# Attention then a cosine-gated MLP on one core: three score tiles to a visit in three rotating PSUM slots, each quad's AV product in one burst, and the last MLP pair of a stage in halves

## The chip, the cores and the metric

The kernel runs on one core of one Trainium2 chip. The metric is the device time of one execution in microseconds; lower is better. A core has five engines that run their own instruction streams and wait for each other through semaphores: TensorE (PE: matrix products, with PEld for its weight loads), ScalarE (ACT), VectorE (DVE), GpSimd (POOL) and SyncE (SP, here only a queue that issues DMAs).

## The reference

```
q, k, v: (8, 12, 448, 64) float32;  tau = 0.1
q_n = q / (norm(q) + 1e-6);  k_n = k / (norm(k) + 1e-6)
attn = softmax(q_n @ k_n.T / tau)             per batch and head, 448 x 448
x = (attn @ v), heads joined                  (3584, 768)
h = x @ w_in                                  (768, 2048)
out = (h * cos(h)) @ w_out                    (2048, 768), float32
```

## The kernel before

**Units.** A *quad* is four heads of one batch element; there are 24 quads (NQ), three per batch element (QB). Its keys are cut into 7 blocks of 64 (NJ). One *score event* `scores(g)` (L551) is four 64x64 matmuls (L560) that fill two neighbouring PSUM banks, and one ScalarE exponential over 128x896 (L567) that writes the tile E[g % NE]. One *AV step* `attend(g)` (L570) is four 64x64 matmuls (L577) that multiply such a tile with V and accumulate over the 7 blocks in banks X and Y (4 and 5); after the seventh, VectorE copies them to AVs (L586). `sums` (L630) gets the softmax denominators of two quads with 128x32 matmuls (L642) into one bank; ScalarE inverts them with a logarithm and an exponential into Zs (L649, L651), sends them to a scratch tensor in DRAM (rscr, L652), SP's queue reads them back spread over partitions (R, L658), and GpSimd multiplies AVs by R into xT (L662; for quad 5 VectorE does).

**Getting q and k ready.** `norm_a` squares q and k on GpSimd (L450) and sums them on VectorE (L454); `norm_b` takes the inverse norm on ScalarE (L480 to L493) and scales q and k on GpSimd (L501); `turn` transposes both with DMAs on SP's queue (L544), from quad 4 on. Loads of q and k are also on SP's queue, those of v and the weights on GpSimd's, the output's stores on SP's.

**The MLP.** A batch element is a *stage* c, 0 to 7. MLP-in: eight pairs of 128 hidden units, twelve matmuls each (`m1_part`, L676, 128x448) into a pair of banks; `m1` (L683) makes h*cos(h) of both at once with two ScalarE and two VectorE operations (L689, L691, L693, L695) into gT. MLP-out (`m2`, L698): for every tile of 128 tokens and half of the columns, 16 matmuls (L704, 128x384) into bank 6 or 7, copied out by VectorE (L722) and stored. A stage has 6 or 8 such half tiles, so 96 or 128 of these matmuls. cos runs on another ScalarE table than the exponential; `table` (L371) loads the one that is needed.

**Order.** TensorE runs in the program's order. The first three quads run ahead of the MLP; the others are spread over the MLP-out phases of stages 0 to 5 (`QUADS`, L731: 5, 4, 3, 3, 3, 3 quads). There the main loop (L916 to L989) lays out the half tiles' matmuls in `items`; `fill(n)` emits n of them, and between the fills `group` (L754) emits a *visit*: one score event, then `flush_av` (L739), which does the AV steps of the visit before, then the second score event. Seven events make four visits per quad. Score events alternate between two slots, bank pairs 0 and 2. For two output tiles at once (three in the last two stages) the first 16 matmuls are cut at 0, 10, 12, 14 and interleaved (`cuts`, L945). The order on the other four engines is not written out: `Planner` (L22) lays all operations out in time with the estimated durations that each `op` call gives, and takes from it each engine's order and the semaphore waits. `lead` makes an operation more urgent, `keep` holds a queue to the program's order.

The AV step of a stage's last visit is flushed in the next stage's MLP-in phase (L934).

Of the kernel before, what the change touches and what calls it, by code (L numbers as in the profile page):

```python
# [271 lines left out]
def bass_cosine_attention__then__act_gcu_kernel(  # L272
# [19 lines left out]
    FIRST = 3  # L292
# [11 lines left out]
    NE, NV, NA = 17, 4, 4  # L304
# [17 lines left out]
    Zs = ring("Zs", 2, [128, S], F32)  # L322
# [228 lines left out]
    def scores(g):  # L551
# [3 lines left out]
        u, bs, es = qd % 2, 2 * (g % 2), g % NE  # L555
# [14 lines left out]
    def attend(g):  # L570
# [17 lines left out]
    Z, LEAD = 6, 15.0  # L588

    def spread(qd, j0, j1):  # L590
# [14 lines left out]
        if j1 < NJ:  # L605
            return
        summed.add(qd)
        act("exp", 0.815, lambda e: e.activation(ar[s].ap(), two(Z), ACT.Ln, bias=0.0, scale=1.0), r=pair(Z), w=[("ar", s)])
        act("exp", 0.83, lambda e: e.activation(ar[s].ap(), ar[s].ap(), ACT.Exp, bias=0.0, scale=-1.0),  # L609
            r=[("ar", s)], w=[("ar", s)])  # L610

    def scale_x(qd):
        b, c0, s = qd // QB, 2 * (qd % QB), qd % 3
        op("dve", 1.01, lambda e: e.tensor_tensor(xT[b % 2].ap()[:, c0:c0 + 2, :], two(X), ar[s].ap(), ALU.mult),
           r=pair(X) + [("ar", s)], w=[("x", b % 2, qd % QB)])
# [12 lines left out]
    rounds, spared = [0], []  # L628

    def sums(quads, bk):  # L630
# [3 lines left out]
        z = n % 2  # L634
# [3 lines left out]
        def mm(e):  # L638
# [9 lines left out]
        zz = Zs[z].ap()[0:32 * np_, :]  # L648
        act("exp", 0.44, lambda e: e.activation(zz, bank(bk, S, 0, 32 * np_), ACT.Ln, bias=0.0, scale=1.0),  # L649
            r=whole(bk), w=[("Zs", z)], lead=LEAD)  # L650
        act("exp", 0.47, lambda e: e.activation(zz, zz, ACT.Exp, bias=0.0, scale=-1.0), r=[("Zs", z)], w=[("Zs", z)], lead=LEAD)  # L651
        op("act", 0.6, lambda e: e.dma_start(rscr.ap()[8 * n:8 * n + rows, :], Zs[z].ap()[0:32 * np_:16, :]),  # L652
           r=[("Zs", z)], w=[("rs", n)], dma=("rs", z), moves=0.05, lead=LEAD)
        for i, qd in enumerate(quads):
            u, sl, b = qd % 2, qd % NA, qd // QB
            for r in range(2):
# [5 lines left out]
            op("dve" if late else "pool", 1.02 if late else 2.04, lambda e, u=u, sl=sl, b=b, c0=c0: e.tensor_tensor(  # L662
                xT[b % 2].ap()[:, c0:c0 + 2, :], AVs[sl].ap(), R[u].ap(), ALU.mult),
                r=[("AV", sl), ("R", u, 0), ("R", u, 1)], w=[("x", b % 2, qd % QB)], lead=LEAD)
# [18 lines left out]
    def m1(c, pr, bk):  # L683
# [3 lines left out]
        bs = pair(bk)  # L687
# [3 lines left out]
        op("dve", 1.005, lambda e: e.scalar_tensor_tensor(ar[s].ap(), ar[s].ap().bitcast(I32), -2.0 * math.pi, two(bk),  # L691
# [334 lines left out]
```

## Time and profile before

| what | value |
|---|---|
| time, median of 3 runs | 441.71 us (440.83 to 442.9) |
| the profiled execution | 441.8 us, of which its span is 439.6 us |
| granted TensorE clock over the span | 0.992 |
| score matmuls L560 | x672, 62.1 us busy |
| AV matmuls L577 | x672, 50.4 us busy |
| MLP-in matmuls L676 | x768, 147.7 us busy |
| MLP-out matmuls L704 | x896, 163.4 us busy |
| exponentials L567 | x168, 916 ns each |
| copies of AV sums L586 | x21, 1087 ns each |

Busy times of TensorE overlap each other, since matmuls are pipelined; the distance between the starts of neighbouring ones is what each takes of the queue. The span falls into a start (to 38.6 us, the first three quads) and eight stages, each an MLP-in phase of about 18.5 us and an MLP-out phase of 17 to 43 us, the first six of which contain the attention of later quads.

### The profile page before, as it was taken

To read this page: it belongs to the slowest core of one execution; us is meant where nothing else is said; L and a number is where in the kernel's file an instruction comes from. 1 tells how busy PE (TensorE), PEld (TensorE's weight loads), DVE (VectorE), ACT (ScalarE), POOL (GpSimd) and SP (SyncE) were. 2 spreads that over 40 slices of the span, in tenths; PEclk is the share of its full clock that TensorE was granted. 3 is DMA by queue.
4 is the path that set the end of the run, shared out by engine and by line. 5 is a ranking of instruction groups with operands and counts; after the bars stand their busy time and mean duration, and the time that the engine had idled before them with its cause. 6 is when DMAs were issued, how large, how long until landed. Compare 5 with 4: busy or idle time off the path is not lost.

```text
span 439.6 us, 8369 instructions
## 1 busy us (share of the span) xinstructions
PE 420.1 (96%) x3544; PEld 204.6 (47%) x3544; DVE 254.7 (58%) x300; ACT 315.3 (72%) x434; POOL 211.2 (48%) x145
## 2 busy tenths in 40 slices
PE   5989999988999999999999999999999999999996
PEld 5444543324544345434554444434454445555553
DVE  4674995347863449823696419923585237825931
ACT  4798789896788877788688667888678666815700
POOL 3878727869167694376637682148633120030000
PEclk9699999999999999999999999999999999999999
DMA  7999996999919969188933994075912611051022
GB/s 253 233 251 227 261 196 92 233 223 208 146 41 240 240 172 213 37 206 123 265 89 80 241 210 141 1 171 150 259 35 48 154 43 30 0 159 36 1 71 73
DMA packets 70941, 64.34 MB, mean 146 GB/s; under 512 B 40100, under 2 KB 63224, under 8 KB 70904
## 3 DMA queue, kind: packets, MB, share of 16 engines
q1 hardware_dynamic: 57824, 51.30, 46.6%
q0 software_dynamic: 12288, 11.80, 18.2%
q10 hardware_dynamic: 792, 0.71, 0.5%
q8 instruction: 28, 0.46, 0.4%
q14 instruction: 9, 0.07, 0.1%
HBM read 55.25 MB, written 11.16 MB: 151 GB/s over the span
## 4 chain that ended last, share of the span: by engine, by line
PE 83%; ACT 9%; DVE 3%; issue 2%; POOL 2%; ACTq 1%; POOLq 0%
PE PS L676 33%; PE PS L704 31%; PE PS L560 7%; PE PS L577 6%; ACT E L567 6%; PE PS L642 4%; DVE n L454 1%; ACT Zs L651 1%; ACT Zs L649 1%; ACTq L652 1%; PE PS L599 1%; PE PS L623 1%; POOL xT L662 0%; DVE gT L695 0%; ACT ar L609 0%
## 5 line engine op out<-in xcount | busy, mean ns | idle before, releaser
L704 PE MATMUL PS<-W,gT 128*128 128x384 bf16 x896 | 163.4, 327 | 1.1 <-DVE osb L722 1.0
L567 ACT ACTIVATE E<-PS 128x896 bf16<-128x896 f32 x168 | 144.8, 916 | 27.0 <-PE PS L560 23.8
L676 PE MATMUL PS<-xT,W 128*128 128x448 bf16 x768 | 147.7, 353 | 1.2 <-POOL xT L662 1.2
L704 PEld LDWEIGHTS PS<-W,gT 128*128 128x128 bf16 x896 | 80.1, 98 | 80.7 <-issue 29.0
L676 PEld LDWEIGHTS PS<-xT,W 128*128 128x128 bf16 x768 | 74.3, 98 | 72.0 <-POOL xT L662 1.6
L689 ACT ACTIVATE ar<-PS 128x896 int32<-128x896 f32 x64 | 58.2, 910 | 45.1 <-PE PS L676 45.1
L691 DVE SCALAR_TENSOR_TENSOR ar<-ar,PS 128x896 f32<-128x896 int32 x64 | 69.2, 1083 | 29.0 <-ACT ar L689 29.0
L722 DVE COPY osb<-PS 128x384 f32<-128x384 f32 x54 | 29.2, 554 | 86.6 <-PE PS L704 86.5
L662 POOL TENSOR_TENSOR xT<-AVs,R 128x896 bf16<-128x896 f32 x20 | 41.4, 2088 | 67.5 <-DMA R<-rscr 67.4
L695 DVE TENSOR_TENSOR gT<-PS,ar 128x896 bf16<-128x896 f32 x64 | 69.6, 1088 | 1.5 <-ACT ar L693 1.0
L693 ACT ACTIVATE ar<-ar 128x896 f32<-128x896 f32 x64 | 60.6, 946 | 13.1 <-DVE ar L691 13.1
L560 PE MATMUL PS<-qT,kT 64*64 64x448 bf16 x672 | 62.1, 368 | 4.9 <-ACT E L567 4.0
L450 POOL TENSOR_TENSOR sqq<-Qf 128x896 bf16<-128x896 f32 x21 | 35.3, 1679 | 49.3 <-DVE n L454 40.9
L577 PE MATMUL PS<-E,Vb 64*64 64x448 bf16 x672 | 50.4, 353 | 2.1 <-ACT E L567 1.8
L501 POOL TENSOR_TENSOR Qn<-Qf,rr 128x896 bf16<-128x896 f32 x21 | 35.4, 1687 | 29.6 <-ACT rr L493 25.1
L450 POOL TENSOR_TENSOR sqk<-Kf 128x896 bf16<-128x896 f32 (+1 forms) x22 | 36.5, 1659 | 25.9 <-DVE n L454 17.9
L586 DVE COPY AVs<-PS 128x896 f32<-128x896 f32 x21 | 22.8, 1087 | 29.6 <-PE PS L577 29.6
L501 POOL TENSOR_TENSOR Kn<-Kf,rr 128x896 bf16<-128x896 f32 (+1 forms) x22 | 37.5, 1705 | 0.5 <-DVE Qn L501 0.5
L560 PEld LDWEIGHTS PS<-qT,kT 64*64 64x64 bf16 x672 | 18.6, 105 | 38.4 <-issue 15.6
L454 DVE TENSOR_REDUCE n<-sqq 128x14 f32<-128x896 bf16 (+2 forms) x24 | 24.9, 1037 | 5.8 <-POOL sqq L450 5.7
L454 DVE TENSOR_REDUCE n<-sqk 128x14 f32<-128x896 bf16 (+2 forms) x24 | 25.0, 1040 | 5.4 <-POOL sqk L450 5.4
L577 PEld LDWEIGHTS PS<-E,Vb 64*64 64x64 bf16 x672 | 19.3, 106 | 17.5 <-ACT E L567 10.6
(53 smaller groups left out, 175.9 us busy)
## 6 DMA issues: line engine op xcount, KB each, us to landing
Qf<-in_q_dram SPq DMA_DIRECT2D x24, 448.0 KB, 6.0
out_dram<-osb SPq DMA_DIRECT2D x54, 192.0 KB, 3.6
Kf<-in_k_dram SPq DMA_DIRECT2D x23, 448.0 KB, 7.2
R<-rscr SPq DMA_DIRECT2D x42, 224.0 KB, 4.2
Vb<-in_v_dram POOLq DMA_DIRECT2D x24, 224.0 KB, 6.7
W<-in_moe_w_in_dram POOLq DMA_DIRECT2D x4, 768.0 KB, 18.3
W<-in_moe_w_out_dram POOLq DMA_DIRECT2D x4, 768.0 KB, 31.9
Kf<-in_k_dram ACTq DMA_DIRECT2D x1, 320.0 KB, 6.2
```

Source lines behind the costliest of these rows:

```text
L450: op(eng, (1.68 if eng == "pool" else 1.05) * n, lambda e: e.tensor_tensor(dst, src, src, ALU.mult), r=cut(nm + "f", s, part), w=at, after ...
L454: return op("dve", 0.07 + 0.95 * n, lambda e: e.tensor_reduce(out=n2[u].ap()[:, H * w:H * w + H] if part == ALL[0] else jr(n2[u], w, part) ...
L501: lambda e: e.tensor_tensor(n[u].ap()[:, j0:j1].rearrange("p j r d -> p r j d"), f[s].ap()[:, :, j0:j1], rb, ALU.mult),
L560: ins = e.matmul(bank(bs + r, S, 64 * a, 64 * a + 64), kT[u].ap()[64 * r:64 * r + 64, j, a, :], qT[u].ap()[64 * r:64 * r + 64, :, a, :], s ...
L567: act("exp", 0.875, lambda e: e.activation(E[es].ap(), two(bs), ACT.Exp, bias=0.0, scale=INV_TAU), r=pair(bs), w=[("E", es)], chain="E")
L577: ins = e.matmul(bank((X, Y)[a], S, 64 * r, 64 * r + 64), Vb[vs].ap()[64 * a:64 * a + 64, r, j, :], E[es].ap()[64 * a:64 * a + 64, r, :], ...
L676: ins = e.matmul(bank(bk + i2), W1.ap()[:, i, 128 * nb:128 * nb + 128], xT[c % 2].ap()[:, i, :], start=(i == 0), stop=(i == NKC - 1))
L689: op("act", 0.815, lambda e: e.activation(ar[s].ap().bitcast(I32), two(bk), ACT.Identity, bias=0.25, scale=INV2PI), r=bs, w=[("ar", s)])
L691: op("dve", 1.005, lambda e: e.scalar_tensor_tensor(ar[s].ap(), ar[s].ap().bitcast(I32), -2.0 * math.pi, two(bk), ALU.mult, ALU.add), r=bs ...
L693: act("sin", 0.86, lambda e: e.activation(ar[s].ap(), ar[s].ap(), ACT.Sin, bias=GUARD * math.pi / 2.0, scale=GUARD), r=[("ar", s)], w=[("a ...
L695: op("dve", 1.01, lambda e: e.tensor_tensor(gT.ap()[:, 2 * pr:2 * pr + 2, col:col + S], two(bk), ar[s].ap(), ALU.mult), r=bs + [("ar", s)] ...
L704: ins = e.matmul(bank(bk, HW), gT.ap()[:, f, col:col + 128], W2.ap()[:, f, HW * h:HW * h + HW], start=(f == 0), stop=(f == NNB - 1))
```

## The change

Scores are visited in threes across quad borders (`visits_of`); the bank pairs 0, 2 and 4 form one ring of three slots, used in turn by score events and gathers (`slot`). `attend` stays for the first three quads; for the others `gather` does all 28 AV matmuls of a quad in one burst, as the third event of the visit after the one with the quad's last score, into a slot of the ring, with the copy to AVs behind it. The final product of a quad is emitted at its gather if its sums came first. `pace` decides how many MLP-out matmuls stand between visits, from estimates of when slots come free. The E ring has 18 tiles for 17, Zs one buffer for two. The last of the eight MLP pairs of a stage goes through its four elementwise operations in two halves, and the first output tile's matmuls are finished before the second's.

```diff
-    NE, NV, NA = 17, 4, 4
+    NE, NV, NA = 18, 4, 4
-    Zs = ring("Zs", 2, [128, S], F32)
+    Zs = sb("Zs", [128, S], F32)
-    def scores(g):
+    def scores(g, slot=None):
-        u, bs, es = qd % 2, 2 * (g % 2), g % NE
+        u, bs, es = qd % 2, 2 * (g % 2 if slot is None else slot), g % NE
...
-        if j == NJ - 1 and qd >= FIRST:
-            sl = qd % NA
-            op("dve", 1.01, lambda e: e.tensor_copy(AVs[sl].ap(), two(X)), r=pair(X), w=[("AV", sl)])
+    def gather(qd, slot):
+        vs, sl, bs = qd % NV, qd % NA, 2 * slot
+        es = [(NJ * qd + j) % NE for j in range(NJ)]
+        def mm(e):
+            for j in range(NJ):
+                for a in range(2):
+                    for r in range(2):
+                        ins = e.matmul(bank(bs + a, S, 64 * r, 64 * r + 64),
+                                       Vb[vs].ap()[64 * a:64 * a + 64, r, j, :],
+                                       E[es[j]].ap()[64 * a:64 * a + 64, r, :],
+                                       start=(j == 0), stop=(j == NJ - 1))
+            return ins
+        op("pe", 0.188 * NJ, mm, r=[("E", i) for i in es] + [("V", vs)], w=pair(bs), mode="q")
+        op("dve", 1.01, lambda e: e.tensor_copy(AVs[sl].ap(), two(bs)), r=pair(bs), w=[("AV", sl)])
+        gathered.add(qd)
+        if qd in products:
+            products.pop(qd)()
+        if qd + NV < NQ:
+            load_v(qd + NV)
...
+            if qd in gathered:
+                product()
+            else:
+                products[qd] = product
...
-        op("act", 0.815, lambda e: e.activation(ar[s].ap().bitcast(I32), two(bk), ACT.Identity, bias=0.25, scale=INV2PI),
-           r=bs, w=[("ar", s)])
...
+        def some(i0, i1):
+            n = i1 - i0
...
+            op("act", 0.225 + 0.295 * n, lambda e: e.activation(ai, src, ACT.Identity, bias=0.25, scale=INV2PI), r=bs, w=at)
...
+        for part in ((0, 1), (1, 2)) if pr == NNB // 2 - 1 else ((0, 2),):
+            some(*part)
...
-    W, MOST = (1, 1), 9
-    E1, E2 = NNB - 6, NNB - 4
+    E0, E1 = NNB - 2, NNB - 6
...
+    def visits_of(quads):
+        steps = [(qd, j) for qd in quads for j in range(NJ)]
+        out, late = [], []
+        while steps:
+            what, steps = steps[:3], steps[3:]
+            now_, later = late, []
+            for p, (qd, j) in enumerate(what):
+                if j == NJ - 1:
+                    (later if p else now_).extend(x for x in ROUNDS if x[-1] == qd)
+            ended = [qd for qd, j in what if j == NJ - 1]
+            if owed:
+                what.insert(2, (owed.pop(0), None))
+            owed.extend(ended)
+            out.append((what, now_))
+            late = later
+        return out, late
+    def slot():
+        events[0] += 1
+        return (events[0] - 1) % 3
+    def visit(what):
+        for qd, j in what:
+            if j == 0:
+                begin(qd)
+            if j is None:
+                gather(qd, slot())
+            else:
+                scores(NJ * qd + j, slot())
+        for qd, j in what:
+            if j == 0 and FIRST < qd < NQ - 3:
+                norm_a(qd + 3, [o for o in P.ops if o.eng == "dve"][-1:])
+            if j == NJ - 1 and qd + 2 < NQ:
+                turn(qd + 2)
+                if FIRST < qd < NQ - 4:
+                    load_qk(qd + 4)
+    def pace(visits, total, last):
...
+            if fills:
+                fills[-1] = max(3, math.ceil(need / 0.163))
...
+        spare = total - sum(fills)
...
+            run += x + spare / len(fills) if spare > 0 else x * total / sum(fills)
...
-            if pr == 1:
-                flush_av()
...
-        cuts = (0, E1, E2, E2 + 2, NNB)
-        items[0:ahead * NNB] = [(*work[i], f) for a, b in zip(cuts, cuts[1:]) for i in range(ahead) for f in range(a, b)]
+        cuts = [(i, 0, E1) for i in range(ahead)] + [(i, E1, E0) for i in range(ahead - 1)]
+        cuts += [(i, E0, NNB) for i in range(ahead - 1)] + [(ahead - 1, E1, NNB)]
+        items[0:ahead * NNB] = [(*work[i], f) for i, a, b in cuts for f in range(a, b)]
+        def can_sum(p):
+            if ahead == 3:
+                return p >= E1
+            return ahead * NNB <= p < len(items) and 2 <= items[p][2] <= 11
...
+        visits, left = visits_of(range(done, done + QUADS[c]))
...
+        if visits:
+            fill(2 * E1 + (4 if c else 0))
+            fills = pace(visits, len(items) - at[0], 14)
+            for i, (what, rounds_here) in enumerate(visits):
...
+                visit(what)
+                due.extend(rounds_here)
+                n = fills[i]
+                while due and not any(can_sum(p) for p in range(at[0], at[0] + n)):
+                    n += 1
+                fill(n)
+            if done == NQ:
+                gather(owed.pop(0), slot())
+                due.extend(left)
+            else:
+                carried = left
```

More of the change, by code (lines that the diff above doesn't have):

```diff
@@ L626, in stir @@
         op("pe", 0.19 * n, mm, r=[("E", g % NE), "zeros"], w=pair(Z), mode="q")
-    rounds, spared = [0], []
+    rounds, spared, gathered, products = [0], [], set(), {}
     def sums(quads, bk):
@@ L954, in fill @@
                 t, h, f0 = items[at[0]]
[L955 to L959 removed]
+                if due and can_sum(at[0]):
+                    sums(due.pop(0), 13 - cur[0] if ahead == 2 else n0 + 1)
                 f1 = f0
@@ L964, in fill @@
                     n -= 1
-                    if due and f1 == 2:
+                    if due:
                         break
```

169 lines of the change are left out of this document (89 added, 80 removed).

## The prediction

> **What bounds the kernel now.** I read the page's busy table first, then the windows of the sixteen phases (cut where the TensorE rows change from L676 to L704 and back), then the TensorE timeline inside one phase, last the ScalarE and GpSimd timelines where TensorE waits.
>
> ```profile
> PE 420.1 (96%) x3544; PEld 204.6 (47%) x3544; DVE 254.7 (58%) x300; ACT 315.3 (72%) x434; POOL 211.2 (48%) x145
> ```
>
> TensorE is busy nearly throughout, so the question is what fills its time. The windows (length, then busy time of PE, PEld, DVE, ACT, POOL) of the six attention phases, called V0 to V5 below; the MLP-in phase ahead of each is M0 to M5:
>
> ```profile
> 56.81:100.28 43.47, 39.10 (x429) 15.52 (x428) 24.67 (x33) 37.92 (x57) 27.87 (x19) 1.00 0.98 184
> 118.87:158.38 39.51, 38.78 (x405) 16.99 (x404) 19.25 (x22) 32.77 (x52) 26.49 (x17) 1.00 0.66 161
> 176.96:207.85 30.89, 29.74 (x317) 13.07 (x316) 14.90 (x17) 26.05 (x40) 18.79 (x12) 1.00 0.59 124
> 226.43:259.30 32.87, 32.87 (x321) 15.82 (x320) 15.93 (x19) 26.36 (x40) 21.92 (x14) 1.00 0.66 158
> 278.05:308.95 30.90, 29.75 (x317) 13.08 (x316) 13.83 (x16) 26.14 (x40) 17.12 (x11) 1.00 0.53 123
> 327.53:360.81 33.28, 33.28 (x325) 15.84 (x324) 12.07 (x16) 25.17 (x32) 7.46 (x4) 1.00 0.34 78
> ```
>
> V3 and V5 are pure TensorE. V2 and V4 have ScalarE close behind (26 of 31). V0 is near ScalarE's limit: 37.9 of 43.5, with the exponentials only starting 4.8 into it. Inside V3, the timeline by start (start, length, line, form, count) gives the price of a visit:
>
> ```profile
> 246.64 1.64 PE L704 MATMUL PS<-W,gT 128*128 128x384 bf16 x9
> 248.20 0.38 PE L560 MATMUL PS<-qT,kT 64*64 64x448 bf16 x4
> 248.42 0.55 PE L577 MATMUL PS<-E,Vb 64*64 64x448 bf16 x8
> 248.90 1.64 PE L704 MATMUL PS<-W,gT 128*128 128x384 bf16 x9
> ...
> 251.16 1.64 PE L704 MATMUL PS<-W,gT 128*128 128x384 bf16 x9
> 252.72 0.38 PE L560 MATMUL PS<-qT,kT 64*64 64x448 bf16 x4
> 252.94 0.55 PE L577 MATMUL PS<-E,Vb 64*64 64x448 bf16 x8
> 253.32 0.36 PE L560 MATMUL PS<-qT,kT 64*64 64x448 bf16 x4
> 253.61 1.48 PE L704 MATMUL PS<-W,gT 128*128 128x384 bf16 x8
> 255.01 0.38 PE L560 MATMUL PS<-qT,kT 64*64 64x448 bf16 x4
> 255.22 0.55 PE L577 MATMUL PS<-E,Vb 64*64 64x448 bf16 x8
> 255.60 0.36 PE L560 MATMUL PS<-qT,kT 64*64 64x448 bf16 x4
> 255.90 1.47 PE L704 MATMUL PS<-W,gT 128*128 128x384 bf16 x8
> ```
>
> From start to start: nine L704 and four events (an event is four 64x64 matmuls, a score or an AV step) take 253.61 - 251.16 = 2.45; eight and four take 2.29, so an L704 is 0.16. Nine and three take 248.90 - 246.64 = 2.26, so an event is 0.19. What is left, 2.45 - 1.44 - 0.76 = **0.25, is the price of one visit**, whatever is in it. Check on V3: 128 x 0.16 + 41 events x 0.19 + one sum (seven steps, 1.33, and 0.25 for its own switches) + 12 visits x 0.25 = 32.85; the window has 32.87. V5 with 42 events and 13 visits gives 33.29 against 33.28. The same sum is 38.09 for V1 (39.51: 1.4 of waits), 29.31 for V2 and V4 (30.9: 1.6 of waits), and 37.7 for V0 (43.47: 5.8 of waits). V0's end shows two of its waits:
>
> ```profile
> 93.22 1.69 POOL Qn L501
> 94.91 1.64 POOL sqq L450
> 96.72 1.43 issue
> 98.15 2.09 POOL xT L662
> 100.28 4.71 PE PS L676 x24
> ```
>
> In the chain of waits M1 starts when GpSimd's product has written xT; TensorE's last matmul before it began near 98.9.
>
> **The change, part by part.** *Fewer visits.* Scores go three to a visit across quad borders: V0 has 35 scores in 12 visits (20 before), V1 28 in 10 (16), V2 to V5 21 in 7 each (12, 12, 12, 13). At 0.25 that is 2.0, 1.5, 1.25, 1.25, 1.25, 1.5.
>
> *AV in a burst.* The matmuls are the same 7 x 0.19 = 1.33 per quad. A quad's gather comes one visit after its last score, so V1 to V4 have 28, 21, 21, 21 AV steps (27, 20, 20, 20 before), V0 28 (34), V5 28 (21) and one visit of its own at the end. The single AV step that each M1 to M5 now contains disappears: those windows are 18.59, 18.58, 18.58, 18.75, 18.58 against 18.17 for M6, which has none; together 2.2 less. The burst's three-slot ring lets ScalarE have three tiles in hand instead of two; the fourth event of a visit reuses the first's slot, and the two scores' 0.4 plus the burst's 1.33 is longer than one exponential and its hand-over, some 1.3 (score to exponential 0.43 at 237.35, then 0.86), so it should not wait.
>
> *AVs copy.* The slot of a gather is free only after VectorE's copy (L586, 1.09). The next to use it is the second event of the next visit, about 0.6 + 0.16 x 6 to 10 matmuls = 1.6 to 2.2 after the burst; hand-over and copy are 1.3. The cover is 0.3 to 0.9 of VectorE delay; if a 1.08 reduction (L454) has just begun, up to 0.8 is left over. Both ends are 0 and 21 x 0.8 = 17; VectorE is half idle in these phases, so I take 0.5 in all.
>
> *Transposes.* SP's two transposes for quad q+2 wait for quad q's last score and land some 6.4 after it (score 67.55, second transpose issued 69.82, 4.1 to landing). The gap to their reader was 9.65 (67.55 to 77.2). It is now, at the worst position (last score first in a visit), two periods and 0.4: V2 (28.25 - 3.9) / 7 x 2 + 0.4 = 7.4. So 1.0 of slack, from which SP's other issues in front (stores 1.2, loads 1.1, R reads behind their 5-us wait on rscr) are paid. Between 0 and some 1.5 at each of six such places; I take 0.3 in all.
>
> *Last MLP pair in halves, and the new order of the first L704.* ScalarE's 448-wide operations are 0.54 (L649) against 0.92 for 896, VectorE's some 0.6 against 1.09: 0.5 more work on each of them per stage. In exchange the first half can start one bank (1.1) earlier. In V3's approach the second gate multiply ended at 230.8 and the exp table load at 230.95; worked through with the halves both come 0.3 to 0.4 earlier. That puts the first exponential at 4.4 instead of 4.6 after the phase's start, limited then by the first scores. The first output tile finishes before the second, so the wait of L704 for VectorE's osb copy in V1, V2, V4 (0.5 each, at 124.56, 182.64, 283.74 in the chain) goes. Both are inside the sums below; without cover the extra work costs 0.5 x 8 = 4 at most.
>
> *Smaller things.* One Zs buffer instead of two costs nothing: rounds are over 10 us apart in most places and their chain is done in about 2. The E ring grows by one. Loads, transposes and stores are as many as before; V's loads follow the gathers and are due four quads later.
>
> **The sum by phase.** TensorE's own need after: V1 36.8, V2 and V4 28.25, V3 31.8, V5 33.4 (five visits fewer in all, but seven AV steps more). ScalarE's need: 21 exponentials at 0.863 (6.04 for seven at 77.64) = 18.1, two sums 3.4, three norms 3.1, start 4.4: 29.0 after V2's start, of which 1.2 may run on into M3, where ScalarE's first operation came 2.5 after the start. So V2's floor is 27.8 to 29.0 beside TensorE's 28.25. I take 29.0 for V2 and V4 (-1.9 each), 37.5 for V1, whose ScalarE floor is 35.0 to 36.2 (-2.0), 31.9 for V3 (-1.0), +0.1 for V5. V0: ScalarE needs 35 x 0.863 + 3.4 + 3.7 from 61.6 on and ends near 98.9 in any case; and M1 waits for the chain sum (84.7), rscr, R, product, whose sum needs quad 5's exponentials. It stands after 24 scores instead of 23, ScalarE loses about 1 less on the way: I take -0.3, with -3 and +1 as ends. M1 to M5: -2.2. Together -9.2; +0.8 for copies and transposes: **-8.4. 441.8 - 8.4 = 433.4 us** (span 431.2). The profiled execution's 441.8 is 0.1 over the median of the runs, 441.71, so the two are taken as one.
>
> **Rivals.** (A) *ScalarE takes it back.* Where the exponentials set the pace a cheaper visit only makes TensorE wait. For it: V0's 5.8 and V2's 1.6 of waits now; against: ScalarE was idle 5 of 31 in V2. Then V0, V2, V4 gain nothing, V1 1.0, and 2.2 + 1.0 + 1.0 - 0.1 = 4.1 remain: 437.7. The Trainium skill, "TensorEngine Tiling (Array Packing)", section PSUM Bottleneck, says that a packed TensorE can leave the PSUM evacuation as the limit; for V0 the trace agrees (37.9 busy of 43.5).
>
> (B) *V0 is released too.* If sum and products come earlier, V0 gives 2 to 3 more and the +0.8 stays out: about 430. Against: R landed some 10 us after the sum.
>
> (C) *The transposes come late.* 1.5 at six places is 9.0 against 9.2: 441.6, no change. For it: SP waits 5.5 at a time for rscr. Against: in V1 to V5 the periods are long.
>
> (D) *Slower: the gather's slot.* If VectorE's copy regularly stands behind another operation, the second score of the next visit waits, and with it everything on TensorE. It decides from 9.2 / 21 = 0.44 per gather on. With 0.7 each it is 14.7 - 9.2 = 5.5 more: 447.3. For it: reductions and osb copies come in pairs. Against: VectorE is busy 15 of 32 in V3, and the copy waited for nothing but L577 before.
>
> **How the numbers follow.** Forecast 0.58 (own range 430.5 to 436.5), A 0.17, B 0.06, C 0.07, D 0.12. About 0.5% (2.2 us) is what a measurement can tell from no change. Faster is the forecast, A and B: 0.81; same C: 0.07; slower D: 0.12. The range goes from 429 (below B) to 440.5, leaving out D and most of C.
>
> **What would show it.** Right: 50 visits of L560 outside the first three quads; 0.25 a visit; M1 to M5 at 18.2; V3 near 31.9, V2 near 29.0; M1 starting within 1 us of 100.3. Wrong: L560 waiting on AVs (D) or on qT and kT (C); V2 and V4 still over 30.5 with ScalarE over 90% from its first exponential (A); a GpSimd or SP order that makes a later M phase wait for xT.

## The result, and the profile after

The changed kernel takes 443.89 us (median of 9 runs, 442.65 to 445.58) against 441.84 (9 runs, 440.35 to 442.92) for the kernel before on the same chip: a ratio of **1.005 [1.003, 1.007]**, half a per cent slower, where 433.4 had been forecast. The profiled execution took 444.6, its span is 442.8.

The first line is the page's busy table, the others are the windows of V0 to V5 (stretch and length, then busy time of PE, PEld, DVE, ACT, POOL, the granted clock, the DMA share, GB/s):

```profile
PE 414.5 (94%) x3544; PEld 212.9 (48%) x3544; DVE 255.2 (58%) x316; ACT 314.7 (71%) x450; POOL 211.2 (48%) x145
```

```profile
56.92:99.32 42.40, 36.75 (x405) 16.80 (x404) 23.56 (x33) 37.62 (x59) 27.88 (x19) 1.00 1.01 182
118.57:160.94 42.37, 39.62 (x438) 19.10 (x436) 20.21 (x25) 34.77 (x57) 29.88 (x20) 1.00 0.72 162
179.10:207.44 28.34, 27.44 (x294) 13.67 (x293) 16.21 (x20) 24.68 (x41) 18.06 (x12) 1.00 0.43 102
225.60:258.42 32.82, 32.06 (x326) 16.80 (x325) 17.04 (x22) 26.48 (x42) 20.91 (x13) 1.00 0.53 124
276.61:311.81 35.20, 30.79 (x322) 14.87 (x321) 14.84 (x19) 24.73 (x42) 18.10 (x13) 0.95 0.57 114
329.97:364.33 34.36, 33.60 (x354) 17.44 (x352) 13.63 (x19) 25.06 (x34) 7.46 (x4) 1.00 0.35 76
```

TensorE has 5.6 us less to do (414.5 for 420.1) and the span is 3.2 longer: the saving is there, and waits have eaten it. V4 stands out, 4.4 above its own busy time and at a lower clock. One sum (28 matmuls, 1.58 us) moved from V2 to V1, so these two are read together: 70.71 for 70.40 before, where 66.5 was forecast.

All phases, from the starts of the first matmuls of each, in us (the runs in the right-hand columns are explained below):

| phase | before | forecast | changed | e3 | e7 | e9 | e10 | e11 | e15 |
|---|---|---|---|---|---|---|---|---|---|
| V0 + M1 | 62.06 | 61.3 | 61.65 | 69.76 | 67.50 | 61.95 | 61.04 | 61.33 | 60.95 |
| V1 + V2 | 70.40 | 66.5 | 70.71 | 70.69 | 70.16 | 68.56 | 66.88 | 70.70 | 66.99 |
| V3 | 32.87 | 31.9 | 32.82 | 32.81 | 36.22 | 32.76 | 32.38 | 32.81 | 32.38 |
| V4 | 30.90 | 29.0 | 35.20 | 31.78 | 28.78 | 30.05 | 34.17 | 31.80 | 30.14 |
| V5 | 33.28 | 33.4 | 34.36 | 34.36 | 37.34 | 33.16 | 33.92 | 34.36 | 33.92 |
| M2 to M5 | 74.49 | 72.7 | 72.67 | 73.18 | 72.64 | 74.49 | 73.64 | 73.49 | 73.34 |

TensorE's own need in V1 to V5, by the prices of the prediction, is 162.9 before and 158.5 after; so **4.6 us of waits became 14.6**. The prediction had taken 160.8 for these five phases, that is 2.3 of waits. This difference of 12.3, less the 0.8 that stood in the forecast apart from the phases, for copies and transposes, is the miss: the span is 442.8 where 431.2 was forecast, 11.6 more.

Phase by phase, these waits (length less TensorE's own need, each sum counted where it stands, rounded) are:

| waits, us | V1 and V2 | V3 | V4 | V5 | together |
|---|---|---|---|---|---|
| before | 3.0 | 0.0 | 1.6 | 0.0 | 4.6 |
| changed | 5.7 | 1.0 | 7.0 | 1.0 | 14.6 |
| run 7 below, visits of two | 4.7 | 1.8 | 1.1 | 1.4 | 9.0 |
| run 11 below, V4's transposes in time | 5.6 | 1.0 | 3.6 | 1.0 | 11.2 |
| run 15 below, both causes out | 1.9 | 0.6 | 1.9 | 0.5 | 4.9 |

The waits view of the changed kernel (engine, line, what it waited for; total us, times, longest; rows of PE and PEld can count one wait twice):

```profile
DVE AVs L600 <- PE PS L593: 46.5, 19, 7.7
...
ACT Zs L670 <- PE PS L663: 8.1, 8, 2.1
...
PEld PS L663 <- ACT E L567: 4.0, 4, 1.7
...
PEld PS L663 <- DVE osb L758: 2.8, 3, 1.3
...
PE PS L560 <- DMA kT<-Kn: 2.1, 1, 2.1
...
PEld PS L560 <- DVE AVs L600: 0.6, 3, 0.2
```

New are waits of a sum (L663) for an exponential or for the bank that an osb copy (L758) holds, and a single one of 2.1 for a transpose. ScalarE in turn waits for the sums: 8.1 in eight, against 1.7 in two (L649) before. The copy of AVs waits for TensorE and hardly ever the other way round, 0.6 in all: the slower rival, D, did not happen in this kernel.

V4's transpose, in the timeline of SP's queue and then that of TensorE (start, length, line, form, count; in brackets the idle time before and what ended it):

```profile
285.59 1.10 SPq L764 DMA_DIRECT2D out_dram<-osb  x2
290.86 2.39 SPq L679 DMA_DIRECT2D R<-rscr  x4
293.34 1.26 SPq L544 DMA_TRANSPOSE qT<-Qn  x1
294.65 1.35 SPq L544 DMA_TRANSPOSE kT<-Kn  x1
```

```profile
297.68 0.57 PE L560 MATMUL PS<-qT,kT 64*64 64x448 bf16 x8
300.37 0.38 PE L560 MATMUL PS<-qT,kT 64*64 64x448 bf16 x4 [2.12 <-DMA kT<-Kn]
300.69 2.23 PE L740 MATMUL PS<-W,gT 128*128 128x384 bf16 x8
302.84 0.96 PE L560 MATMUL PS<-qT,kT 64*64 64x448 bf16 x8
```

Four reads of R stand in front of the transposes, and SP waited 4.1 for rscr before it could issue them. The second transpose was issued at 294.65; the score that reads it should have started at 298.06 (two events of 0.19 behind 297.68) and starts at 300.37. The eight L740 behind it take 2.15 from start to start, where eight took 1.40 before (253.61 to 255.01): the granted clock had fallen (last section). Before, the same reads stood in front of the same transposes:

```profile
289.29 2.39 SPq L658 DMA_DIRECT2D R<-rscr  x4
291.97 1.24 SPq L544 DMA_TRANSPOSE qT<-Qn  x1
293.25 1.31 SPq L544 DMA_TRANSPOSE kT<-Kn  x1
```

There SP's wait for rscr (3.4) was over early. The transposes need the last score of an earlier quad; it came at 291.54, when the reads were nearly issued, and the first transpose went 0.43 behind it. In the changed kernel this score comes at 290.07 and the first transpose 3.27 behind it, since the reads were only now being issued. The reader stood 7.43 behind the second transpose's issue (300.68) and would stand 3.41 behind it now.

The price of a visit is read in V3:

```profile
237.69 0.76 PE L560 MATMUL PS<-qT,kT 64*64 64x448 bf16 x12
239.10 1.51 PE L663 MATMUL PS<-E,sel 128*32 128x448 bf16 x28 [0.64 <-ACT E L567]
...
245.43 1.96 PE L740 MATMUL PS<-W,gT 128*128 128x384 bf16 x11
247.32 0.76 PE L560 MATMUL PS<-qT,kT 64*64 64x448 bf16 x12
248.01 2.29 PE L740 MATMUL PS<-W,gT 128*128 128x384 bf16 x13
250.23 0.57 PE L560 MATMUL PS<-qT,kT 64*64 64x448 bf16 x8
250.63 1.49 PE L593 MATMUL PS<-E,Vb 64*64 64x448 bf16 x28
251.95 0.36 PE L560 MATMUL PS<-qT,kT 64*64 64x448 bf16 x4
252.25 1.96 PE L740 MATMUL PS<-W,gT 128*128 128x384 bf16 x11
```

248.01 - 245.43 = 2.58 holds eleven L740 and three events, 1.76 + 0.57, and leaves **0.25**; 252.25 - 248.01 = 4.24 holds thirteen and ten events, 2.08 + 1.90, and leaves 0.26. There are 50 visits with scores outside the first three quads, as forecast. The second row shows the new kind of wait: the sum stands directly behind the visit whose three scores complete its round, and has to wait for the last of their exponentials.

The start of V1, ScalarE and then VectorE:

```profile
121.63 0.58 ACT L725 ACTIVATE ar<-ar 128x448 f32<-128x448 f32 x1 [0.95 <-DVE ar L723]
122.23 1.28 ACT L371 ACT_TABLE_LOAD   x1
123.60 0.92 ACT L567 ACTIVATE E<-PS 128x896 bf16<-128x896 f32 x1
```

```profile
119.46 0.61 DVE L723 SCALAR_TENSOR_TENSOR ar<-ar,PS 128x448 f32<-128x448 int32 x1
119.99 1.08 DVE L728 TENSOR_TENSOR gT<-PS,ar 128x896 bf16<-128x896 f32 x1
120.99 0.61 DVE L723 SCALAR_TENSOR_TENSOR ar<-ar,PS 128x448 f32<-128x448 int32 x1
```

VectorE puts the whole gate product of the pair before (1.08) between the two halves of the last pair, so ScalarE waits 0.95 for the second half. The first exponential comes 123.60 - 118.57 = 5.03 after the phase's start, in V4 too (281.64 - 276.61); it was 4.6, and 4.4 was forecast.

### The profile page after: what moved, and what is told of

Read it like the earlier page. It is cut to its first block, busy times and chain, and to the rows that moved or that the text cites. A ratio compares the mean times of both kernels' runs of the same rounds, so it can differ in the third digit from the quotient of the medians.

```text
span 442.8 us, 8413 instructions
## 1 busy us (share of the span) xinstructions
PE 414.5 (94%) x3544; PEld 212.9 (48%) x3544; DVE 255.2 (58%) x316; ACT 314.7 (71%) x450; POOL 211.2 (48%) x145
## 4 chain that ended last, share of the span: by engine, by line
PE 70%; ACT 16%; DVE 8%; issue 3%; DMA 1%; ACTq 0%; POOL 0%; SPq 0%; POOLq 0%; DVEq 0%
PE PS L704 30%; PE PS L740 24%; ACT E L567 11%; PE PS L560 5%; PE PS L593 5%; PE PS L663 4%; DVE gT L728 3%; DVE ar L723 2%; DMA kT<-Kn 1%; ACT L371 1%; DVE n L454 1%; ACT ar L722 1%; DVE osb L758 1%; ACT Zs L672 1%; PE PS L645 1%
## 5 line engine op out<-in xcount | busy, mean ns | idle before, releaser
L740 PE MATMUL PS<-W,gT 128*128 128x384 bf16 x896 | 157.8, 328 | 0.1
L704 PE MATMUL PS<-xT,W 128*128 128x448 bf16 x768 | 146.9, 353 | 0.9 <-DVE xT L685 0.9
L740 PEld LDWEIGHTS PS<-W,gT 128*128 128x128 bf16 x896 | 83.3, 98 | 70.0 <-issue 18.0
L704 PEld LDWEIGHTS PS<-xT,W 128*128 128x128 bf16 x768 | 74.6, 98 | 71.8 <-DVE xT L685 1.3
L722 ACT ACTIVATE ar<-PS 128x896 int32<-128x896 f32 (+1 forms) x72 | 59.3, 828 | 47.2 <-PE PS L704 47.2
L723 DVE SCALAR_TENSOR_TENSOR ar<-ar,PS 128x896 f32<-128x896 int32 (+1 forms) x72 | 70.1, 979 | 31.5 <-ACT ar L722 31.5
L685 POOL TENSOR_TENSOR xT<-AVs,R 128x896 bf16<-128x896 f32 x20 | 41.6, 2084 | 79.5 <-DMA R<-rscr 79.2
L725 ACT ACTIVATE ar<-ar 128x896 f32<-128x896 f32 (+1 forms) x72 | 61.8, 863 | 13.8 <-DVE ar L723 12.8
L758 DVE COPY osb<-PS 128x384 f32<-128x384 f32 x54 | 29.6, 552 | 72.5 <-PE PS L740 72.3
L728 DVE TENSOR_TENSOR gT<-PS,ar 128x896 bf16<-128x896 f32 (+1 forms) x72 | 70.3, 983 | 1.8 <-ACT ar L725 1.0
L560 PE MATMUL PS<-qT,kT 64*64 64x448 bf16 x672 | 52.7, 369 | 9.9 <-ACT E L567 6.0
L560 PEld LDWEIGHTS PS<-qT,kT 64*64 64x64 bf16 x672 | 16.0, 105 | 40.0 <-ACT E L567 19.4
L593 PE MATMUL PS<-E,Vb 64*64 64x448 bf16 x588 | 32.1, 355 | 2.9 <-ACT E L567 2.8
L593 PEld LDWEIGHTS PS<-E,Vb 64*64 64x64 bf16 x588 | 16.4, 108 | 15.9 <-ACT E L567 5.2
```

The costliest lines, as they stand in the source:

```text
L560: ins = e.matmul(bank(bs + r, S, 64 * a, 64 * a + 64), kT[u].ap()[64 * r:64 * r + 64, j, a, :], qT[u].ap()[64 * r:64 * r + 64, :, a, :], s ...
L593: ins = e.matmul(bank(bs + a, S, 64 * r, 64 * r + 64), Vb[vs].ap()[64 * a:64 * a + 64, r, j, :], E[es[j]].ap()[64 * a:64 * a + 64, r, :], ...
L704: ins = e.matmul(bank(bk + i2), W1.ap()[:, i, 128 * nb:128 * nb + 128], xT[c % 2].ap()[:, i, :], start=(i == 0), stop=(i == NKC - 1))
L722: op("act", 0.225 + 0.295 * n, lambda e: e.activation(ai, src, ACT.Identity, bias=0.25, scale=INV2PI), r=bs, w=at)
L723: op("dve", 0.07 + 0.47 * n, lambda e: e.scalar_tensor_tensor(a, ai, -2.0 * math.pi, src, ALU.mult, ALU.add), r=bs + at, w=at)
L725: act("sin", 0.225 + 0.32 * n, lambda e: e.activation(a, a, ACT.Sin, bias=GUARD * math.pi / 2.0, scale=GUARD), r=at, w=at)
```

## The experiments

Ratios are to the kernel before, measured on the same chip, with 95% intervals. The orders of the other four engines come out of the planner's estimates, so an edit of one number can move operations in several queues; where it did, that is said.

**1. The last pair whole again, in the changed kernel.**

```diff
-        for part in ((0, 1), (1, 2)) if pr == NNB // 2 - 1 else ((0, 2),):
+        for part in ((0, 2),):
```

> The changed kernel with one part undone: the last MLP pair of a stage goes through its four operations whole again. In the changed kernel the exp table load of the fifth MLP-out phase starts 3.66 after the phase began, against 3.24 in the kernel before, and the fourth event of the first visit waits 0.3 for its slot. Theory (the halves delay ScalarE, because VectorE puts a whole gate multiply between them): table load back at 3.2, first exponential 0.4 earlier in six phases, 1 to 2.5 us less than the changed kernel, near 442. Rival (the halves help, because the first output tile is finished sooner): 1 to 2 us more, near 445.5.

445.79, 1.0087 [1.0063, 1.0111]: no faster without the halves. The first exponential comes at 5.39 instead of 5.03, and the first gather of each of V1 to V5 waits for the whole pair's gate product, since the third event of a stage's first visit takes the banks in which that pair lies (a row of 5.5 in five, up to 1.1). V1, V2, V3 and V5 are each 0.5 to 0.8 longer. Only V4 is shorter, 32.72: R's reads stand ahead of its transposes as in the changed kernel, but both come 0.8 earlier in the phase, the score waits 1.3 for kT instead of 2.1, and the granted clock stays at 1.00 (0.95 over V4 in the changed kernel). So the halves do not cause the loss; with three rotating slots they save that wait.

**2. The sums six matmuls later.**

```diff
-            return ahead * NNB <= p < len(items) and 2 <= items[p][2] <= 11
+            return ahead * NNB <= p < len(items) and 6 <= items[p][2] <= 11
...
+                first = min(6, fills[i])
+                fill(first)
                 due.extend(rounds_here)
-                n = fills[i]
+                n = fills[i] - first
```

> The changed kernel with the sums of softmax denominators put at least six MLP-out matmuls after the visit before them, and not before the sixth matmul of an output tile. Theory (sums stand too close behind the last score's exponential or the bank's copy, and TensorE waits in front of them: 0.5, 1.5, 0.7, 1.0, 0.6 and 0.7 us in the changed kernel's phases V1, V1, V3, V4, V4, V5, 5.0 in all): 4 to 5 us less, near 439.5, V3 at 32.1. Rival (those waits stand for ScalarE's backlog, and the same time is waited for at the next score or the next phase): V3 and V5 0.7 less each, the rest unchanged, near 442.4.

446.92, 1.0117 [1.0089, 1.0145]. The sums hardly wait any more (0.8 in all by the rows of PE, for 4.2), yet V3 is 33.25 (32.82) and V5 34.65 (34.36): there the time comes back in front of the next scores, 0.7 each. That ScalarE's pace lies under it is argued here and tested in runs 9 and 10. V4 is another matter. It is 31.51, 3.7 shorter, although R's reads still stand ahead of its transposes: its sums wait 0.2 for a bank instead of 1.5, the score 1.4 for kT instead of 2.1, and the granted clock stays at 1.00. V1 to V5 are 3.1 shorter together; what makes the run slower lies outside them, V0 above all (45.76, in another order).

**3. The planner told that the scratch write lands 3.5 us later.**

```diff
-            o.end = self.land(e, avail[e], o.moves) if o.dma else s + o.dur + o.lat
+            o.end = self.land(e, avail[e], o.moves) + (3.5 if o.dma[0] == "rs" else 0.0) if o.dma else s + o.dur + o.lat
```

> The changed kernel with one number of the planner altered: the write of the inverse sums to DRAM is taken to land 3.5 us later than it assumed, so that SP's queue gets the reads of R behind the transposes in V4 instead of ahead of them. No instruction is added. Theory (V4 is 4.3 us longer than before because transposes stood behind R's 4.1 us wait): the 2.3 us wait for kT goes and V4 falls from 35.2 to 32 or below, total near 441. Rival (the transposes are only the last to arrive; POOL or ScalarE hold the same scores): V4 stays above 34 and the total within 1 us of 443.9.

448.98, 1.0146 [1.0115, 1.0176], but V4 is 31.78, 3.4 less: with the transposes ahead of R's reads its wait is gone. The loss is elsewhere: V0 is 4.8 and M1 3.3 longer, in another order. M1 waits for xT: for 1.4 at its start and 2.6 in it, since VectorE's product of quad 5 (L685) takes 5.04 us there, for 1.91 in the changed kernel. GpSimd runs products of its own beside it; that these slow it is not shown.

**4. The three together.** The three diffs above in one kernel.

> The three alterations together: whole last pair, sums later, scratch write assumed to land later. If the three are separate costs: 7 to 9 us less than the changed kernel, 435 to 437, which is below the kernel before. If they hide one ScalarE limit: about as much as the best of the three alone, 440 to 441.

458.65, 1.0365 [1.0328, 1.0402], with V0 at 50.88 and M5 at 22.38. The edits are not independent: each moves the planner's order for the others. Nothing follows for the causes, except that single places have to be changed from here on.

**5. Denominators without urgency from the third round on.**

```diff
+        LEAD = 15.0 if n < 2 else 0.0
```

> The changed kernel with one number altered: from the third round of sums on (those of stages 1 to 5, whose xT is needed a whole stage later) the sum's two ScalarE operations, its scratch write, R's reads and the product get no lead of 15 us in the planner. The order of V0 stays. Theory (in V1 to V5 ScalarE is held by each sum's two operations and its DMA issue, 1.8 us ahead of three scores that wait, and V4's transposes by R's reads): V4 at 31.5 or less, each of V1, V3, V5 shorter by 0.5 or more, total near 438. Rival (ScalarE's place in the order does not matter, since slots and bursts set the pace): V4 alone gains 3.4, total near 441.

446.53, 1.0102 [1.0081, 1.0124]: V4 is 30.69, with R's reads behind its transposes, V3 and V5 are unchanged, and V1 is 48.85. There TensorE stands still for 4.3: a score waits for a copy of AVs, and the copy waits 4.4 for GpSimd's product into xT, which had lost its urgency too. So the wait of rival D can arise, though by another way than a busy VectorE. For the question of the sums the run is a miss.

**6. The later landing only for rounds 2 and up, and V1's last sum handed on to V2.**

```diff
+ (3.5 if o.dma[0] == "rs" and o.writes[0][1] > 1 else 0.0)
...
-                    (later if p else now_).extend(x for x in ROUNDS if x[-1] == qd)
+                    (later if p or not steps else now_).extend(x for x in ROUNDS if x[-1] == qd)
```

> The changed kernel with the longer scratch landing of the third run applied from the third round of sums on only, and with the sum that stands behind V1's last score (TensorE waits 1.5 for that exponential) handed on to V2, where the kernel before has it. Theory: V0 and M1 as in the changed kernel (61.7 together), V4 31.8, V1 and V2 together 1.4 shorter than 70.7: total near 439. Rival (V2 pays for the sum as much as V1 did): V1 and V2 stay at 70.7, total near 441.

445.81, 1.0063 [1.0031, 1.0095]. V1 falls to 39.34 and V2 rises to 31.21: 70.55 together, as before the edit. Moving a sum by one phase gains nothing. M2, 19.84, waits 1.5 for xT, and M3, 18.97, 0.6 for a bank that a gate product (L728) frees late.

**7. Visits of two scores instead of three.**

```diff
-            what, steps = steps[:3], steps[3:]
+            what, steps = steps[:2], steps[2:]
```

> The changed kernel with two scores to a visit instead of three, all else as it is: 76 visits instead of 50, four more in each of V1 to V5 and six in V0. If TensorE's price of a visit is what the change saves: 0.25 x 20 = 5 us more outside V0, near 449. If the bursts of three in a ring of three slots give the saving back by starving ScalarE and then waiting for it: the waits shrink by as much, and the total stays within 1.5 us of 443.9 or falls.

447.25, 1.0121 [1.0099, 1.0144]. In V1 to V5, 20 more visits are 5.0 more of TensorE's own need, and the five phases last 172.5 instead of 173.1: the waits fell by 5.6. But all of this is V4's, 7.0 to 1.1, where no reads of R stand ahead of the transposes now and one sum has moved elsewhere; in the other four phases the waits are 7.9 for 7.6 (table above). Against run 11, whose transposes are in time too, visits of three are 2.8 shorter in the five phases (169.7), of the 5.0 that they save TensorE. So the run does not show that three scores at a time cause the waits; by this comparison somewhat over half of the saving stays once V4's order is right. (What it loses against the changed kernel lies in V0, 49.16.)

**8. The same number of matmuls between all visits**, in place of `pace`.

```diff
-            fills = pace(visits, len(items) - at[0], 14)
+            rest = len(items) - at[0]
+            fills = [rest * (i + 1) // len(visits) - rest * i // len(visits) for i in range(len(visits))]
```

> The changed kernel with the MLP-out matmuls shared out evenly over the visits of a phase instead of by the estimate of when slots come free. In V3 the first five gaps have 18, 12, 17, 11, 13 and the last 22; evenly each has 14 or 15. If the spacing is what makes ScalarE idle (4.4 of 26.5 us between V3's first and last exponential): V1, V3 and V5 lose 0.5 to 1.5 each and the total falls to about 441. If the estimate is sound: waits of scores grow where a gather's visit follows, total 445 or more.

448.56, 1.015 [1.0126, 1.0174]; V3 and V5 are the same to a hundredth, V4 is 35.93 with a wait of 3.0 for kT, V0 is 48.28, and the median is 4.7 above the changed kernel's. The distribution that `pace` chooses matters in V0 and not where the waits of V3 and V5 arise.

**9 and 10. Exponentials of half the columns**, in the kernel before and in the changed one; the softmax of the other half is left out, and every order stays as it is.

```diff
-        act("exp", 0.875, lambda e: e.activation(E[es].ap(), two(bs), ACT.Exp, bias=0.0, scale=INV_TAU),
+        w = S if qd < FIRST else S // 2
+        act("exp", 0.875, lambda e: e.activation(E[es].ap()[:, :, 0:w], two(bs)[:, :, 0:w], ACT.Exp, bias=0.0, scale=INV_TAU),
```

> The kernel before, with every exponential from quad 3 on over half of its columns (the other half of the tile keeps what it held; the softmax of those columns is left out), all orders and waits as they were. ScalarE loses some 0.38 us in each of 147 exponentials. V1 to V5 were 167.5, of which TensorE's own need is 162.9 and waits 4.6. Theory (ScalarE set those waits): V1 to V5 fall to 163 to 165. Rival: they stay above 166.

> The changed kernel with the same cut: exponentials from quad 3 on over half of the columns, order untouched. V1 to V5 were 173.1, TensorE's own need by my sum 158.5, waits 14.6. Theory (visits did become cheaper by the forecast amount, and ScalarE's pace, not the price of a visit, took it back): the waits fall by 7 or more outside V4's wait for kT, V1 to V5 to 161 to 166, and this kernel is shorter than the kernel before with the same cut by what V1, V3 and V5 save. Rival (the sums, slots and transposes cost the time whatever ScalarE's speed): V1 to V5 stay above 169 and the kernel stays the slower of the two.

439.08, 0.9943 [0.9919, 0.9967] before, and 437.01, 0.9901 [0.9866, 0.9936] changed. With ScalarE relieved the changed kernel has the lower median, but the intervals overlap. V1 to V5 lose 5.7 us (173.1 to 167.4), those of the kernel before 3.0 (167.5 to 164.5); 167.4 lies between what the theory (161 to 166) and the rival (above 169) had expected. In these phases TensorE's waits for an exponential, by the rows of PE, fall from 5.2 to 1.0 in the changed kernel and from 1.8 to 0.4 in the one before. V4 of the changed kernel stays at 34.17: its wait for the transpose is no matter of ScalarE's.

**11. The later landing for one round only**, the one in V4.

```diff
+ (3.5 if o.dma[0] == "rs" and o.writes[0][1] == 7 else 0.0)
```

> The changed kernel with the longer scratch landing told to the planner for one round of sums alone, the one whose R reads stood ahead of V4's transposes. V0 to M4 stay as they are. Theory: V4 from 35.2 to 31.8, little after it, total 440 to 441, 0.3% below the kernel before. Rival (the product of that round comes so late that M5 waits, and the order of the later phases pays): M5 and later give back 1 or more, total 442 or above.

441.60, 1.0005 [0.9985, 1.0025]: as fast as the kernel before, 2.3 below the changed one. SP's queue in V4:

```profile
291.01 1.24 SPq L544 DMA_TRANSPOSE qT<-Qn  x1
292.30 1.30 SPq L544 DMA_TRANSPOSE kT<-Kn  x1
...
294.80 3.50 SPq L679 DMA_DIRECT2D R<-rscr  x4
```

Counted from V4's start (277.12 here), the first transpose goes at 13.89 instead of 16.73, and the reads of R, with their wait, stand behind both. V4 is 31.80, 3.4 shorter, and in runs 3, 6 and 13, with the same order in V4, it is 31.78 to 31.80. From V1 on every other phase is as it was but M5, which is 0.85 longer: TensorE waits there for a bank that a gate product (L728) frees late, as the late R holds up GpSimd, GpSimd the norm of another quad, and this ScalarE's table load, which comes 3.4 after M5's start instead of 1.3. That 3.4 of V4's excess came from the order on SP's queue is shown; how much the old order costs depends on how late the transposes get (V4 was 32.72 and 31.51 with it in runs 1 and 2).

**12. The halves alone, in the kernel before**, with the new order of the first output tiles (core of the diff).

```diff
+        for part in ((0, 1), (1, 2)) if pr == NNB // 2 - 1 else ((0, 2),):
+            some(*part)
...
+        cuts = [(i, 0, E1) for i in range(ahead)] + [(i, E1, E9) for i in range(ahead - 1)]
+        cuts += [(i, E9, NNB) for i in range(ahead - 1)] + [(ahead - 1, E1, NNB)]
```

> The kernel before with the second part of the change alone: the last MLP pair in halves, and the first output tile's matmuls finished before the second's; visits, slots and AV steps as before. Theory (the wait of TensorE for the osb copy, 0.5 in each of V1, V2 and V4, goes, and the second gate multiply is off the path in both): 1 to 1.5 us less than the kernel before, 440.5 to 441. Rival (the exp table load comes 0.4 later, as in the changed kernel): V1, V2 and V4 keep their length and V0 grows by 0.4, total within 0.5 of the kernel before or slower.

441.85, 1.0003 [0.9982, 1.0024]. V1 to V5 are 167.8 for 167.5. The wait for the osb copy in the middle of the first tiles is gone and stands, with 0.3 in the rows of PE, in front of the sum; V1, V2 and V4 are 0.1 to 0.2 shorter, and V3 and V5, which had no waits, 0.4 longer each. By itself this part is worth nothing.

**13. As 11, with 2.0 in place of 3.5.**

> As the eleventh run, with 2.0 us instead of 3.5 for that one round, which puts its R reads right behind V4's two transposes and ahead of the next loads. Theory (the eleventh run's M5 waited 0.85 for a product that came late because of the two loads in front): V4 31.8 as there, M5 18.2 again, total near 440.7, 0.2% below the kernel before. Rival (M5 waits for something else): M5 stays at 19.0, total 441.6.

442.46 (441.52 to 445.74, 13 runs), 1.001 [0.9988, 1.0032]. R's reads stand right behind V4's transposes; V4 is 31.80 and M5 18.16, both as expected, and yet the median is not below run 11's. The profiled execution, 445.74, spent 48.49 in V0: TensorE stood still from 64.8 to 70.36 in front of quad 4's first score. That quad's second transpose had held SP's queue for 6.5 us, from 52.46 on, but it did so in the changed kernel too (6.49, from 52.26 on), where the same score waited only 1.8 (by the profile for an exponential). That its landing, at differing times, is what the score waits for is argued from the order; the profile names no releaser.

**14. As 11, and the scratch write issued from SP's queue instead of ScalarE's** from the third round on.

```diff
-        op("act", 0.6, lambda e: e.dma_start(rscr.ap()[8 * n:8 * n + rows, :], Zs.ap()[0:32 * np_:16, :]),
+        op("act" if n < 2 else "sp", 0.6 if n < 2 else 0.5, lambda e: e.dma_start(rscr.ap()[8 * n:8 * n + rows, :], Zs.ap()[0:32 * np_:16, :]),
```

> As the eleventh run, and from the third round of sums on the write of the inverse sums is issued by SP's queue instead of ScalarE's, which was held 0.57 by each ahead of waiting exponentials. Theory (ScalarE's time behind a sum is what V1, V2 and V4 wait for): V1 1.0 to 1.5 shorter (three sums), V2 and V4 0.5 each, V3 and V5 unchanged, total near 439.5. Rival (SP's queue holds the transposes behind the new write, which waits for ScalarE): a phase grows by 1 to 4, total above 442.

440.95 (12 runs), 0.9978 [0.9958, 0.9998]: 0.2% below the kernel before, the fastest version of the whole computation here. V1 is 41.80 for 42.36 and V4 31.04 for 31.80 in run 11, V2 is unchanged; M5 gives nothing back (18.21). For V1 1.0 to 1.5 less had been expected, for V2 0.5.

**15. Both causes out:** run 13's order and run 10's half exponentials.

> The thirteenth kernel with the exponentials of the tenth (half of the columns from quad 3 on): transposes in time and ScalarE faster, both causes out together. If these two hold the forecast saving: V1 to V5 at 163 to 164 against 164.5 of the kernel before with the same cut, the M phases 1.8 less, total 432 to 434 against 439.1. If something else holds it: V4 stays above 33 or the total above 436.

434.10, 0.9829 [0.9787, 0.987]; 5.0 below run 9, the kernel before with the same cut. V1 to V5 take 163.4, so 14.6 of waits became 4.9.

## Why the prediction was wrong

**The step that failed is the sum by phase**, in its passage from TensorE's own need to the time taken. The need itself was right, 158.5 for V1 to V5 both forecast and after; what was set on top, 2.3 us, became 14.6. The prediction compared TensorE's total in a phase with ScalarE's total and took the larger. But three scores in 0.69 us hand ScalarE 2.6 us of exponentials at once, and a sum, a gather or a fourth event directly behind them needs the last of these: in V1 to V5 TensorE waits 5.2 us for exponentials by the rows of PE, 1.4 of it in front of one sum in V1, where the kernel before waits 1.8 in all. Totals can fit where the order cannot. That it is the number of three that does this, and not the place of sums and gathers, is not shown: with visits of two these waits are 4.7 (run 7).

- *Fewer visits*: right in number (50) and price (0.25 to 0.26).
- *AV in a burst*: M2 to M5 fell to 18.16, as forecast. M1 rose instead, 19.25, for VectorE's product of quad 5 (L685). "It should not wait", said of the fourth event, was wrong: in the first visit of each phase it waits 0.3, since the first exponential is late.
- *AVs copy*: 0.5 taken, 0.6 in the waits view. Rival D is out for this kernel.
- *Transposes*: the mechanism of rival C, at one place instead of six. The term taken was 0.3 in all, its upper end 1.5 at a place; V4 alone lost 3.4 (runs 3 and 11), 2.3 of it waiting and the rest at a lower clock, which the working had no term for. The working had the 5-us wait of SP for rscr in it, but as something that the slack of 1.0 pays; here it put the first transpose 3.27 behind the score on which it depends, for 0.43 before.
- *Halves*: the wait for osb went from its place to the sum's (run 12), and the first exponential came 0.4 later, not 0.2 earlier, since VectorE put a whole gate product between the halves. The halves are not the cause of the loss; without them V1, V2, V3 and V5 are longer (run 1).
- *ScalarE*, rival A: its mechanism is there, in another form than its own test. It asked for V2 and V4 over 30.5 with ScalarE busy over 90% from its first exponential on. V2 came out at 28.34, having lost a sum to V1; V4, with its transposes in time, is still 31.80 (run 11), but ScalarE has 6.1 us of idle time there between its first and last exponential (9.3 in the changed kernel). What the runs show is a price for the exponentials' length: 5.7 us in V1 to V5 go when they are halved (run 10), and in V3 and V5 a moved sum brings its wait along (run 2). The Trainium skill, "TensorEngine Tiling (Array Packing)", section PSUM Bottleneck, says that after such a speed-up of TensorE the emptying of PSUM may become the bottleneck. Run 10 agrees; with V1, V3 and V5 at 5 to 6.5 us of such idle time, though, it is more the hand-over that limits than ScalarE's total.
- *V0*: -0.3 forecast, -1.1 in the profile, -0.4 with M1. V0 differs by several us between orders that are alike there, so no more is read from it. (The 37.7 of own need for V0 before does not come out of the prices: 96 L704, 69 events, 20 visits, one and a half sums and the first transposes make about 37.0, so its waits were some 6.5. Nothing else hangs on this.)

**What explains the 12.3.** The order on SP's queue in V4 is 3.4 and the exponentials' length 5.7, each by taking it out alone; both out bring 14.6 to 4.9 (run 15). The 2.3 that the prediction had taken were put there for ScalarE, so most of the 4.9 has no place in its sum. Nor is all of the 5.7 new: the kernel before loses 3.0 by the same cut. Of the 10.0 by which the waits grew from kernel to kernel (4.6 to 14.6), 3.3 are left with both causes out (1.6 to 4.9). The trace shows sums in V4 waiting 1.5 for banks that osb copies hold, in run 15 as in the changed kernel, where VectorE has the AVs copy and two reductions in front of them. Run 2, with the sums six matmuls later, brought this wait to 0.2 and V4 to 31.51, but kT came sooner and the clock stayed up there too, so its share is not known.

**What remains open.** With both causes out the change brings 5.0 of the forecast 8.4, but half of the columns were then cut from the kernel before as well, whose own waits fell to 1.6; in V1 to V5 alone the two differ by 1.1 only (164.5 and 163.4). The rest of the profiled difference is M1 to M5 (1.6), V0 (0.6) and the start (1.1), which lasts anything from 37.1 to 39.6 us in these runs, whatever the kernel. How much of the change could be had with full exponentials and a better order isn't shown. Nor is it settled why V0 lasts 42 to 49 us.

## What to carry to other kernels

When a tuned engine's work is bundled into fewer, larger bursts, add up not only what each engine has to do in a phase but walk one burst through: how long the next engine needs for it, and what stands directly behind it that needs its last piece. When work moves in time, look at what stands ahead of a producer in the DMA queue, a wait of that queue above all: 3.4 us of it cost nothing as long as it was over before the producer's own input came. To find out whether an engine sets the pace, shorten its operations with all orders kept; edits of a planner's numbers move everything else too. And when a total of waits falls, see in which phase it fell before giving the edit the credit (run 7).

## What the runs showed of the hardware

**A short standstill of TensorE costs a second time.** The windows around V4's wait (columns as above; the granted clock is third from the end):

```profile
301.00:302.00 1.00, 1.00 (x6) 0.50 (x4) 0.00 (x0) 0.72 (x1) 1.00 (x1) 0.63 1.07 387
302.00:303.00 1.00, 1.00 (x7) 0.31 (x9) 0.00 (x0) 0.00 (x0) 1.00 (x2) 0.50 1.09 422
303.00:304.00 1.00, 1.00 (x16) 0.42 (x16) 0.00 (x0) 0.52 (x1) 1.00 (x1) 0.50 0.15 31
304.00:305.00 1.00, 1.00 (x20) 0.55 (x16) 0.00 (x0) 1.00 (x2) 1.00 (x2) 0.67 1.03 197
```

TensorE had stood still for 2.3 us (by the starts of its matmuls), until 300.37; the clock falls to 0.50 only when it is at work again, and for some 3.5 us. By these windows 1.7 us of work are lost; V4 was lengthened by 1.1 besides the wait (3.4 less 2.3). Run 10 shows the same in V4 after 2.4; in run 13 the clock fell near 69, within the standstill of 5.7, and stayed at 0.50 until 75, five us after its end. In V4 of runs 1 and 2, where the waits view gives 1.3 and 1.4 for this wait (2.1 in the changed kernel), the clock stayed at 1.00. Runs 10 and 15 have standstills of 2.5 and 2.9 in V0 without a drop, so it doesn't come every time. The Trainium skill, "TensorE: Matmul & The Clock Gate", section "What's actually happening", gives an idle window of about 3.4 us, free-running; that the drop comes after some standstills and not after others fits a free-running window, but a standstill of 2.3 was enough here.

**A DMA transpose can hold its queue.** Its issue took 1.2 to 1.4 us in V4, but 3.1 and 6.5 for two in a row at 49 to 59 us of the changed kernel, directly behind four loads of q and k. From its issue to the score that reads it 5.7 us passed in V4 (294.65 to 300.37).
